# Attention and a gated feed-forward block: two written orders of steps joined into one, with buffers and banks named at each step

## The chip, the cores and the metric

The kernel runs on one core of a Trainium2 chip. The metric is device time in microseconds of one execution. A core has a matrix engine (TensorE, here PE, with its weight loads shown apart as PEld), VectorE (DVE), ScalarE (ACT) and GpSimd (POOL), and SyncE (SP), which issues the DMA transfers. Each engine works through its own queue in program order; an instruction waits in its queue until the instructions of other engines that it depends on have finished.

## The reference

The input is `q`, `k`, `v` of shape (8, 8, 576, 64): 8 batches, 8 heads, 576 positions, 64 features. Keys and values are averaged over groups of 8 positions, so each head attends to 72 of them. The result, as 4608 tokens of 512 features, goes through RMS normalization and a gated feed-forward block with 1536 inner features.

```python
k_p = k.reshape(B, H, Sp, pool, D).mean(axis=3)
v_p = v.reshape(B, H, Sp, pool, D).mean(axis=3)
scores = scale * np.matmul(q, k_p.transpose(0, 1, 3, 2))
attn = softmax(scores)
x = np.matmul(attn, v_p)            # then as (4608, 512)
xn = x / np.sqrt(np.mean(x * x, axis=-1, keepdims=True) + 1e-06) * rms_g
g = xn @ w_gate
out = (g * (1.0 / (1.0 + np.exp(-g))) * (xn @ w_val)) @ w_out
```

`softmax(scores)` stands here for the four lines that subtract the maximum, take the exponential and divide by the sum.

## The kernel before

**Precision.** The weights arrive as 64-bit numbers. Each is taken apart into a high and a low part, both in the 32-bit format that the profile calls fp32r, and activations are split in the same way. A product of two such numbers takes three matmuls: high by high, high by low, low by high.

**Tiling.** The 4608 tokens form 9 blocks of 512 (block 0 to 8). The 1536 inner features are 12 slices of 128, written in base 36 (0 to b) in the names of steps. For block i and slice f there are three groups of twelve matmuls with 512 columns each:

- `mm1` for the gate (L802 to L813, step `mg` or `_g`) and for the value (`me` or `_e`), into one PSUM bank each,
- `mm2`, the output product (L840 to L853, `mo` or `_o`), which adds into four banks that belong to the block for all its twelve slices.

Between them stand `gate` (`gt`, ACT: Silu out of the bank), `val` (`vl`, DVE: times the value bank), `act_hi` (`hi`, ACT: high part) and `act_lo` (`lo`, DVE: low part). `hl` and the activation `act` have one buffer each, `hh` has two.

Blocks 5 and 6, and 7 and 8, are computed in pairs by a scheme with seven products instead of eight (L752 to L764, `pr`): for each slice, seven groups of six matmuls, with sums and differences of activations (`ys`, `yh`, `yl`) and of weights. The parts of the weights (`wd`, `wt`, `wf`, `wh`, `wl`, `ws`) are prepared during earlier blocks, stored to device memory, and each comes back by a DMA into one of eight ring buffers just before its product (`rl`, L741 to L750). Ahead of `mo` for the second block of a pair (6 and 8), the first block's `mo`, in two halves (`mp`), is mixed with the products. The steps `cp`, `u2`, `sa`, `u3`, `c2`, `sw`, `v2`, `v1`, `va`, `vb` combine the products on ACT and DVE.

**Attention** of batch b, head pair p: loads (`lk`, `lq`, `lv`), pooling (`pk`, `pv` on DVE), scores on PE (`sc`, two banks), maximum and difference (`mx`, `sb`, DVE), exponential (`ex`, ACT), sums (`sm`, DVE), division (`nm`, POOL), a transposition (`tr`, DVE) with twelve small DMAs that place its parts (`dm`), the value product on PE (`av`, two halves), copies (`xc`, `xd`), squares (`sq`, `jn`). When a batch is done, sums of squares (`sh`, `sl`, `rm`), roots and scaling (`rt`, `rc`, `rs`) follow. Batches 0 and 1 take a path of their own, with transposes on PE; their steps are single letters.

**The order.** Nothing reorders the instructions: `manual_schedule` emits the steps as they are written. There are two written orders. `ORDER` (L52) holds batch 0, the splitting of all weights (`l` to `h`, `w`, `W`), block 0 and batch 1. Then a loop copies block 0's four output tiles and stores them. Then `LATER` (L88) holds everything else. The function `run` (L871) reads a step, a colon and bank numbers if there are any: `sc20:01` puts the scores in banks 0 and 1. Without a number a step has a fixed bank: the gate 2, the value 3, a block's output 4 to 7, products 2 and 3.

**Buffers.** Tiles of the pool `sb2` have two buffers, used in turn. The ring's eight buffers are used in turn as well. A step that takes a buffer or a bank waits for the last reader of what lay there before. `o_copy` (`ev`, L855: DVE for tiles 0 and 2, ACT for 1 and 3) copies an output tile out of its bank into one of the two `out` buffers, and `o_store` (`st`) issues the transfer.

Of the kernel before, what the change touches and what calls it, by code (L numbers as in the profile page):

```python
# [85 lines left out]


LATER = """  # L88
lv21 sc20:01 kt1 mg10 lk21 mx200 sb200 mx201 ex200 sb201 me10 gt10 sm200 nm200 ex201 mg11 vl10 hi10 sm201 lo10 nm201
me11 pv21 gt11 pk21 tr20 lq21 mo10 vl11 lv22 dm20 hi11 lo11 mg12 sc21:01 gt12 me12 mx210 sb210 mx211 ex210 lk22  # L90
sb211 mo11 vl12 ex211 sm210 hi12 lo12 nm210 sm211 av200:0 pk22 av201:1 nm211 xc200 mg13 lq22 xc201 xd20 tr21 sq20
pv22 dm21 me13 gt13 sc22:01 wt0 vl13 hi13 mo12 mx221 sb221 wf00 lo13 ex221 wf01 lk23 mx220 mg14 wf02 sb220 wh01
sm221 wf03 ex220 wd0 wh03 sm220 wl01 lv23 nm221 ws01 av210:0 gt14 nm220 pk23 av211:1 wl03 me14 lq23 xd21 xc210 ws03
xc211 mo13 vl14 hi14 pv23 wh04 wl04 mg15 lo14 ws04 wh02 wl02 sc23:01 ws02 sq21 tr22 gt15 jn21 me15 dm22 mx230 sb230
mx231 ex230 sb231 mo14 vl15 ex231 sm230 hi15 lo15 nm230 sm231 mg16 nm231 lk30 tr23 me16 gt16 dm23 av220:0 vl16
av221:1 pk30 xc220 hi16 mo15 xd22 xc221 sq22 lo16 jn22 mg17 lq30 lv30 wt1 me17 gt17 wf10 sc30:01 vl17 wd1 wf11 wh11
hi17 pv30 wl11 mo16 lk31 wh13 wf12 ws11 mx301 lv31 wl13 lo17 wf13 ws13 mx300 mg18 sb300 sb301 ex300 av230:0 ex301
sm300 gt18 av231:1 sm301 nm300 me18 xd23 nm301 pk31 xc231 xc230 pv31 lq31 wh14 wh12 wl14 mo17 vl18 wl12 ws14 hi18
ws12 tr30 sq23 jn23 lo18 mg19 dm30 sh2 sl2 me19 gt19 rm21:0 vl19 rm20:1 rt21 mo18 hi19 rc21 rt20 mg1a lv32 rs21
av300:0 lo19 av301:1 xc300 rc20 gt1a me1a xd30 rs20 xc301 sq30 wt2 sc31:01 vl1a mo19 lk32 mx311 hi1a wf20 mx310 wf21  # L100
lo1a wh21 wf22 wh23 sb310 mg1b wl23 sb311 wd2 ex310 pv32 wf23 ws23 wl21 pk32 ex311 ws21 sm310 me1b gt1b lq32 sm311
nm310 nm311 mo1a tr31 xh22 xh21 xl22 dm31 xh20 xl21 xh23 xl20 wh22 wh24 wl22 xl23 sc32:01 wl24 vl1b kt2 mg20 mx320
hi1b sb320 lo1b ex320 mx321 sb321 me20 lk33 gt20 lv33 sm320 ws22 ws24 nm320 ex321 mo1b vl20 hi20 pk33 lo20 lq33
av310:0 sm321 ev13 av311:1 xc310 st13 ev12 nm321 mg21 xc311 xd31 st12 sq31 pv33 jn31 tr32 sc33:01 ev11 gt21 st11
ev10 dm32 me21 mx330 sb330 mx331 ex330 sb331 mo20 vl21 ex331 sm330 hi21 wt3 sm331 lo21 mg22 nm331 st10 nm330 lk40
wf30 me22 gt22 wd3 wf31 tr33 wf32 wh31 dm33 wf33 wh33 av320:0 vl22 wl33 av321:1 xc320 pk40 wl31 hi22 mo21 xd32 xc321
lo22 mg23 lq40 me23 ws33 gt23 ws31 mo22 vl23 hi23 lo23 wh32 wh34 av330:0 wl32 av331:1 xc330 wl34 ws32 mg24 xc331
xd33 ws34 sq32 lv41 jn32 sc40:01 gt24 lv40 me24 lk41 mx400 sb400 mx401 ex400 sb401 pv41 mo23 ex401 vl24 sq33 sm400
hi24 jn33 pv40 mg25 nm400 sh3 lo24 sl3 pk41 me25 gt25 wt4 sm401 lq41 rm30:0 vl25 nm401 rm31:1 rt30 mo24 wf40 tr40
wf41 hi25 rc30 dm40 wf42 rt31 mg26 wh41 wf43 wh43 wl41 lo25 wl43 rs30 sc41:01 gt26 rc31 me26 rs31 wd4 mo25 lk42 ws41  # L110
vl26 ws43 mx411 hi26 sb411 mg27 lo26 ex411 mx410 sb410 ex410 sm411 av400:0 gt27 sm410 nm411 av401:1 nm410 me27 xd40
pk42 xc401 xc400 lq42 sq40 wh42 wh44 wl42 mo26 vl27 wl44 ws42 hi27 ws44 tr41 lv42 sc42:01 lo27 dm41 mg28 mx420 mx421
sb421 sb420 ex421 pv42 me28 gt28 sm421 nm421 mo27 ex420 vl28 lk43 hi28 sm420 lv43 wt5 mg29 lo28 pk43 nm420 av410:0
lq43 gt29 wf50 av411:1 wf51 me29 wd5 xd41 xc410 wf52 pv43 xc411 wh53 wf53 wh51 wl53 sq41 sc43:01 vl29 wl51 ws53 hi29
jn41 ws51 mo28 mx431 lk50 mx430 lo29 mg2a wh52 wl52 wh54 wl54 ws52 ws54 tr42 me2a gt2a sb431 dm42 pk50 ex431 sb430
mo29 vl2a ex430 sm431 hi2a sm430 nm431 lo2a mg2b nm430 tr43 me2b dm43 gt2b mo2a xh33 vl2b xh31 xl33 xh32 xl31 xh30
# [840 lines left out]
```

## Time and profile before

| | |
|---|---|
| time, median of 3 runs | 1022.78 us (1021.83 to 1024.94) |
| span of the profiled execution | 1024.9 us |
| first large matmul of block 0 starts at | 52.39 us |
| last matmul ends at about | 1019.1 us |
| mean granted clock of TensorE | 0.976 |

The profile is that of one execution. The page gives busy time for each engine, the span in slices, the chain of work that ended last, and the costliest groups of instructions. A group is named by its line, engine and operation, what it writes and what it reads (`po<-w,hl` writes `po`), then its count, its busy time, the mean duration of one in ns, and how long its engine was idle just before, with what ended that wait. Matmuls are pipelined, so their durations overlap: the time of one is read from the spacing of their starts.

The large matmuls of a slice all have 512 columns. The profile's lines for them are L811 (`psg`), L852 (`po`) and L763 (`px`, `py`). Attention on PE is L389 (`pss`, scores) and L470 (`psx`, value product).

```
DVE  7899996554783955685485486644655764444432
ACT  6757664553473564454364453322324431211121
PEclk8689999999999999999999999999999999999999
```

These three rows of the page show the span in 40 slices of 25.6 us: busy tenths of DVE and ACT, and the tenths of TensorE's full clock that were granted.

### The profile page before, as it was taken

To read this page: it belongs to the slowest core of one execution; us is meant where nothing else is said; L and a number is where in the kernel's file an instruction comes from. 1 tells how busy PE (TensorE), PEld (TensorE's weight loads), DVE (VectorE), ACT (ScalarE), POOL (GpSimd) and SP (SyncE) were. 2 spreads that over 40 slices of the span, in tenths; PEclk is the share of its full clock that TensorE was granted. 3 is DMA by queue.
4 is the path that set the end of the run, shared out by engine and by line. 5 is a ranking of instruction groups with operands and counts; after the bars stand their busy time and mean duration, and the time that the engine had idled before them with its cause. 6 is when DMAs were issued, how large, how long until landed. Compare 5 with 4: busy or idle time off the path is not lost.

```text
span 1024.9 us, 13861 instructions
## 1 busy us (share of the span) xinstructions
PE 992.1 (97%) x4850; PEld 790.8 (77%) x4850; DVE 632.3 (62%) x1024; ACT 449.7 (44%) x845; POOL 227.2 (22%) x216
## 2 busy tenths in 40 slices
...
DVE  7899996554783955685485486644655764444432
ACT  6757664553473564454364453322324431211121
...
PEclk8689999999999999999999999999999999999999
...
GB/s 313 121 166 180 176 75 58 79 147 139 68 175 136 79 179 104 152 119 145 111 138 154 123 90 105 173 199 153 147 160 147 42 113 154 151 153 149 103 41 42
DMA packets 97076, 134.71 MB, mean 131 GB/s; under 512 B 10224, under 2 KB 60144, under 8 KB 95728
## 3 DMA queue, kind: packets, MB, share of 16 engines
...
q8 instruction: 39, 0.64, 0.3%
...
## 4 chain that ended last, share of the span: by engine, by line
PE 86%; DVE 7%; ACT 3%; issue 1%; DMA 1%; SPq 0%; POOL 0%; ACTq 0%; DVEq 0%; POOLq 0%
PE psg L811 28%; PE po L852 27%; PE py L763 13%; PE px L763 10%; PE pss L389 4%; PE psx L470 3%; DVE wt L257 1%; DVE wt L261 1%; DMA main<-kT 1%; PE pst L446 1%; PE psr L554 1%; DVE hl L838 1%; DVE wt L253 1%; DVE xraw L546 0%; PE psb L578 0%
## 5 line engine op out<-in xcount | busy, mean ns | idle before, releaser
L811 PE MATMUL psg<-xh,w 128*128 128x512 f32 x960 | 304.2, 399 | 2.0 <-ACT act L818 2.0
L852 PE MATMUL po<-w,hh 128*128 128x512 f32 x864 | 225.1, 392 | 0.0
L811 PEld LDWEIGHTS psg<-xh,w 128*128 128x128 f32 x960 | 179.6, 190 | 48.4 <-issue 5.3
L852 PEld LDWEIGHTS po<-w,hh 128*128 128x128 f32 x864 | 163.5, 189 | 34.7
L811 PE MATMUL psg<-xl,w 128*128 128x512 f32 x480 | 188.0, 393 | 0.3 <-DVE xl L641 0.3
L763 PE MATMUL py<-xp,wp 128*128 128x512 f32 x576 | 146.5, 390 | 0.8 <-DVE u L913 0.8
L852 PE MATMUL po<-w,hl 128*128 128x512 f32 x432 | 125.2, 399 | 10.0 <-DVE hl L838 5.1
L763 PEld LDWEIGHTS py<-xp,wp 128*128 128x128 f32 x576 | 108.0, 188 | 24.1 <-DVE u L913 1.2
L763 PE MATMUL px<-xp,wp 128*128 128x512 f32 x432 | 110.2, 390 | 0.0
L811 PEld LDWEIGHTS psg<-xl,w 128*128 128x128 f32 x480 | 91.2, 190 | 20.4 <-DVE xl L641 0.7
L852 PEld LDWEIGHTS po<-w,hl 128*128 128x128 f32 x432 | 79.9, 189 | 32.6 <-DVE hl L838 6.7
L420 POOL TENSOR_TENSOR prob<-prob,sm 128x360 f32<-128x360 f32 x48 | 43.3, 903 | 275.8 <-DVE sm L416 267.5
L763 PEld LDWEIGHTS px<-xp,wp 128*128 128x128 f32 x432 | 80.8, 188 | 17.8 <-ACT xraw L478 0.5
L823 DVE TENSOR_TENSOR act<-act,psg 128x512 f32<-128x512 f32 x60 | 41.0, 683 | 77.4 <-PE psg L811 76.4
L833 ACT CAST hh<-act 128x512 fp32r<-128x512 f32 x84 | 52.1, 621 | 64.4 <-DVE act L823 55.8
L838 DVE TENSOR_TENSOR hl<-act,hh 128x512 fp32r<-128x512 f32 x78 | 57.1, 732 | 32.8 <-ACT hh L833 25.9
L818 ACT ACTIVATE act<-psg 128x512 f32<-128x512 f32 x60 | 35.9, 598 | 67.2 <-PE psg L811 63.6
L818 ACT ACT_TABLE_LOAD x34 | 43.6, 1283 | 33.8 <-DVE hl L838 17.8
L910 DVE TENSOR_TENSOR u<-u,py 128x512 f32<-128x512 f32 x24 | 16.5, 688 | 64.4 <-PE py L763 64.4
L515 POOL TENSOR_TENSOR acc<-acc,sq 128x576 f32<-128x576 f32 x21 | 31.4, 1497 | 99.9 <-ACT sq L509 92.9
L912 ACT ACTIVATE hb<-hb 128x512 f32<-128x512 f32 x24 | 15.2, 632 | 85.8 <-DVE hb L911 85.8
L685 POOL TENSOR_TENSOR wt<-wsum,wt 128x256 fp32r<-128x256 f32 x48 | 38.9, 825 | 51.9 <-ACT wt L681 51.8
(132 smaller groups left out, 1220.8 us busy)
## 6 DMA issues: line engine op xcount, KB each, us to landing
...
```

Of the source, the lines that this page charges most:

```text
L389: nc.tensor.matmul(s["ps", h][:, t * SP:(t + 1) * SP], s["q"][r, o:o + P], s["pk"][r, :], start=True, stop=True)
L420: nc.gpsimd.tensor_tensor(l_pr(h), l_pr(h), sm[:, :, None].broadcast_to([P, len(OFFS2), SP]), ALU.mult)
L470: nc.tensor.matmul(ps[r, :n], s["pv"][:, r], x, start=True, stop=True)
L515: nc.gpsimd.tensor_add(acc[b], acc[b], st[b, p]["sq"])
L685: nc.gpsimd.tensor_sub(y[:, 1], place(f, f"T{k}"), y[:, 0].bitcast(F32))
L763: nc.tensor.matmul(ps[:, :NB], w[:, a, c, :], x[:, b, c, :], start=j == 0 and not more, stop=j == len(todo) - 1, skip_group_check=more)
L811: nc.tensor.matmul(ps[:, :NB], w[:, c, cols], x[c], start=(j == 0), stop=(j == len(todo) - 1))
L818: nc.scalar.activation(t, ps[:, :NB], AF.Silu)
L823: nc.vector.tensor_mul(t, t, ps[:, :NB])
L833: nc.scalar.copy(a, act_in(i, f))
L838: eng.tensor_sub(l, act_in(i, f), hh[i, f].bitcast(F32))
L852: nc.tensor.matmul(po[i][t], x[i, f][:, t * P:(t + 1) * P], w, start=(f == 0 and k == 0), stop=(f == NF - 1 and k == 2))
```

## The change

The two orders become one. Steps that were in `ORDER` have an underscore in front, and the loop behind it is replaced by the steps `ev00` to `ev03` and `st00` to `st03`, which stand among the others. The steps as such, 2,593 of them, are the same before and after. Up to `_g0` of block 0 the order is the same; behind it, it is another. Steps of the two former orders are mixed where block 0 ends.

A step can now name a bank behind a colon for every use of PSUM that has one, `mg` and `me`, products and a block's four output banks too; and behind a slash which of two buffers (or of the ring's eight) its tile takes. The pool `sb2` is gone: `two` takes a tile of `sb1` whose tag ends with the named number.

So that steps of two slices or two blocks can lie between each other, gate, value, activation and product results are kept by block and slice and no longer by "the last one"; and `tokens` takes a block's kept tail only for positions within it.

The loader, the interpreter and the records:

```diff
-    sb2 = ctx.enter_context(tc.tile_pool(name="sb2", bufs=2))
+    taken = []
+
+    def two(shape, dt, tag, name):
+        return sb1.tile(shape, dt, tag=f"{tag}{taken.pop(0)}", name=name)
...
-        w = ring[i, f, k] = sb1.tile([P, 2, 2, P], F32R, tag=RING[len(ring) % len(RING)], name=f"wp{i}_{f}_{k}")
+        w = ring[i, f, k] = sb1.tile([P, 2, 2, P], F32R, tag=RING[int(taken.pop(0))], name=f"wp{i}_{f}_{k}")
...
-        if k in (0, 4):
-            st["X"] = bank(2, f"px{i}_{f}_{k}")
-        elif k in (1, 3, 5):
-            st["Y"] = bank(3, f"py{i}_{f}_{k}")
-        ps = st["Y"] if k in (1, 3, 5, 6) else st["X"]
+        if k in (0, 1, 3, 4, 5):
+            st["XY", i, f, k] = bank(2 if k in (0, 4) else 3, f"pxy{i}_{f}_{k}")
+        ps = st["XY", i, f, {2: 0, 6: 5}.get(k, k)]
...
-        ps = st["psg", 0]
-        t = st["act"] = sb1.tile([P, NB], F32, tag="act", name=f"act{i}_{f}")
+        ps = st["psg", i, f, 0]
+        t = st["act", i, f] = sb1.tile([P, NB], F32, tag="act", name=f"act{i}_{f}")
...
         for step in order.split():
+            step, _, free = step.partition("/")
+            taken[:] = free
             step, _, banks = step.partition(":")
             given[:] = [int(x) for x in banks]
             steps[step[:n]](*(int(x, 36) for x in step[n:]))
...
-        run(ORDER, 1, steps)
-        for t in range(NB // P):
-            o_copy(0, t)
-            o_store(0, t)
...
-        first_phase()
-        later_phase()
+        nc.sync.dma_start(gcol, gain)
+        run(ORDER, 2, {**{"_" + k: v for k, v in first_steps().items()}, **later_steps()})
```

The order where block 0 goes over into block 1, before and after:

```
ORDER: ... Fa B11:1 H10 ia o9 H11 K20 V20 q20 gb:2 La eb:3 Gb oa Fb ib jb t0 t1 t2 t3 ob
       (o_copy and o_store of block 0, tiles 0 to 3)
LATER: lv21 sc20:01 kt1 mg10 lk21 mx200 sb200 mx201 ex200 sb201 me10 gt10 sm200 nm200 ex201 mg11 vl10 hi10 sm201 ...

after: ... _gb _r1 _s1 _B10 _dp _q20 _B11:1 wd5 wd4 _eb _H10 _H11 _ho _wo _La _oa _Gb _Fb sc20:03 _t3 _t0 _t2 wd8
       _t1 _hp mg10 _v20/0 _wp _ib/1 _jb gt10 mx200/1 sb200 lk21 pk21/0 lv21/1 lq21 _ob ev01/1 ev00/0 st01 _V20/0
       ex200 sm200/1 me10:0 vl10 hi10/1 mx201/1 nm200 mg11 st00 sb201 ex201 sm201/1 ev02/0 sc21:01 lo10 me11 ev03/1
       gt11 mo10:5467 ...
```

In the middle, behind slice 5 of block 1 and slice 2 of block 2:

```
before: me15 dm22 mx230 sb230 mx231 ex230 sb231 mo14 vl15 ex231 sm230 hi15 lo15 nm230 sm231 mg16 ... me16 gt16 ... mo15
after:  me15 vl15 me16:0 hi15/0 kt1 tr23/0 lo15 av221:3 xc221 gt16 xd22 mo15
before: me22 gt22 wd3 wf31 tr33 wf32 wh31 dm33 wf33 wh33 av320:0 vl22 wl33 av321:1 xc320 pk40 wl31 hi22 mo21 ... mo22
after:  me22:0 lk40 gt22 av321:1 tr33/1 vl22 hi22/1 lo22 wh33/0 wl33 dm33/0 mg23:3 gt23 av320:2 wf32 xc321 mo22
```

Where block 5 goes over into block 6, and block 7 into block 8:

```
before: pr5b6 av730:0 rl710 v15b av731:1 va5b xc730 xc731 xd73 hi5b sq73 lo5b jn73 mo5b hi60 lo60 sh7 sl7 mo60 hi61
        ev52 ev51 ev50 st52 ev53 st51
after:  pr5b6 av731 xc731 mp5a0 v15b va5b hi5b/1 av730:3 xc730 mp5a1 xd73 sq73/0 jn73 sh7/1 lo5b sl7 mo5b ev52 hi60/0
        rm70:3 lo60 ev53 st53 ev51 ev50 st50 hi61/1 lo61 rm71:1 st52 rt71 rc71 mo60:6470

before: mp7a0 sa7b pr7b3 pr7b4 u37b pr7b5 c27b sw7b mp7a1 v27b vb7b pr7b6 v17b va7b hi7b lo7b mo7b hi80 lo80 mo80 hi81
        ev72 ev71 ev70 st72 ev73 st71
after:  pr7b4:3 lo7a pr7b5:1 c27b v27b mp791 rl7b6/4 pr7b6 v17b pr7b2 mp7a0 sa7b mp7a1 va7b hi7b/1 sw7b lo7b mo7b
        hi80/0 lo80 mo80:2103 ev72 hi81/1 lo81 mo81
```

In the products, an excerpt of slice 2 of block 7:

```
before: pr720 rl730 v171 va71 pr721 rl731 cp72 hi71 pr722 lo71 rl732 u272 mp710 rl733 sa72 pr723 pr724 rl734 u372 pr725
after:  pr720 rl716/2 pr716 mp701 rl721/4 cp72 rl722/5 pr721:1 v171 va71 pr722 hi71/0 lo71 sa72 rl723/6 mp710 pr723:0
        sw71 rl732/2 rl724/4 pr724 rl725/5 u272 pr725
```

More of the change, by code (lines that the diff above doesn't have):

```diff
@@ new lines @@
+_B11:1 wd5 wd4 _eb _H10 _H11 _ho _wo _La _oa _Gb _Fb sc20:03 _t3 _t0 _t2 wd8 _t1 _hp mg10 _v20/0 _wp _ib/1 _jb gt10
+mx200/1 sb200 lk21 pk21/0 lv21/1 lq21 _ob ev01/1 ev00/0 st01 _V20/0 ex200 sm200/1 me10:0 vl10 hi10/1 mx201/1 nm200
+mg11 st00 sb201 ex201 sm201/1 ev02/0 sc21:01 lo10 me11 ev03/1 gt11 mo10:5467 nm201 tr20/0 mx210/0 vl11 mx211/1 sb211
+ex211 wdb lk22 hi11/0 lo11 mg12:3 sb210 ex210 gt12 sm211/1 nm211 st03 wda st02 pv21/1 dm20/1 pk22/0 _J10 me12:1
+sm210/0 mo11 av200/0 xc200 nm210 lv22/1 mg13 lq22 vl12 tr21/0 wd1 wd6 av201:1 hi12/0 xd20 dm21/0 lo12 pv22/0 gt13 me13
@@ new lines @@
+rl5a2/7 u359 c259 v259 sw59 pr596 v159 pr592 sa59 vb59 sc73:01 va59 hi59/0 mx731/1 sb731 ex731 mx730/0 sb730 rl5a0/3
+pr5a0 cp5a ex730 rl5a3/6 rl5a4/5 pr5a1 u25a rl5b1/3 sm731/1 pr5a4:1 nm731 lo59 pr5a3:0 rl5a5/2 rl5b2/6 u35a sm730/0
+nm730 pr5a2 sa5a c25a sw5a pr5b1 pr5a5:0 v25a mp590 rl5a6/7 pr5a6 rl5b0/3 pr5b0 tr73/1 cp5b rl5b3/2 mp591 v15a va5a
+u25b rl5b4/0 vb5a pr5b3:1 u35b hi5a/0 pr5b4:0 rl5b5/1 pr5b5:1 c25b lo5a dm73/0 pr5b2 sa5b v25b pr5b6 av731 xc731 mp5a0
+v15b va5b hi5b/1 av730:3 xc730 mp5a1 xd73 sq73/0 jn73 sh7/1 lo5b sl7 mo5b ev52 hi60/0 rm70:3 lo60 ev53 st53 ev51 ev50
@@ L71 @@
+v27a mp790 vb7a rl7a6/4 pr7b0 cp7b pr7a6 v17a va7a hi7a/0 pr7b1:1 u27b pr7b3:0 u37b rl7b4/1 pr7b4:3 lo7a pr7b5:1 c27b
+v27b mp791 rl7b6/4 pr7b6 v17b pr7b2 mp7a0 sa7b mp7a1 va7b hi7b/1 sw7b lo7b mo7b hi80/0 lo80 mo80:2103 ev72 hi81/1 lo81
+mo81 hi82/0 lo82 mo82 hi83/1 ev73 lo83 mo83 hi84/0 ev70 lo84 mo84 hi85/1 lo85 hi86/0 st72 mo85 lo86 mo86 ev71 hi87/1
+lo87 hi88/0 mo87 lo88 hi89/1 st70 lo89 mo88 hi8a/0 mo89 vb7b st73 hi8b/1 lo8a mo8a st71 lo8b mo8b ev80 ev82 ev83 st83
+st80 ev81 st81 st82
 """
@@ L85 @@
 AHEAD = 12
[L88 to L98, printed above, removed]
@@ L164 @@
-rl700 pr5b4 rl701 u35b rl702 rl703 rl704 pr5b5 c25b rl705 sw5b mp5a1 rl706 v25b vb5b pr5b6 av730:0 rl710 v15b
-av731:1 va5b xc730 xc731 xd73 hi5b sq73 lo5b jn73 mo5b hi60 lo60 sh7 sl7 mo60 hi61 ev52 ev51 ev50 st52 ev53 st51
-lo61 st50 st53 rm71:0 hi62 rm70:1 mo61 rt71 lo62 rt70 rc71 mo62 hi63 lo63 rc70 mo63 hi64 lo64 rs70 mo64 hi65 lo65
-rs71 mo65 hi66 ys73 yh72 yh71 lo66 yl72 mo66 hi67 yh73 lo67 yl71 yh70 mo67 hi68 yl70 lo68 ys74 mo68 hi69 lo69 yh74
-yl73 mo69 hi6a yl74 lo6a ys76 mo6a hi6b lo6b yh76 ys75 mo6b yl76 yh75 yl75 pr700 ev61 ev63 st61 pr701 st63 cp70
@@ L184 @@
-u27b mp7a0 sa7b pr7b3 pr7b4 u37b pr7b5 c27b sw7b mp7a1 v27b vb7b pr7b6 v17b va7b hi7b lo7b mo7b hi80 lo80 mo80 hi81
-ev72 ev71 ev70 st72 ev73 st71 lo81 st70 st73 mo81 hi82 lo82 mo82 hi83 lo83 mo83 hi84 lo84 mo84 hi85 lo85 mo85 hi86
-lo86 mo86 hi87 lo87 mo87 hi88 lo88 mo88 hi89 lo89 mo89 hi8a lo8a mo8a hi8b lo8b mo8b ev83 ev82 ev81 ev80 st83 st82
-st81 st80
-"""
 EXP_SCALE = 1.0 / (POOL * float(np.sqrt(D)))
```

302 lines of the change are left out of this document (160 added, 142 removed).

## The prediction

> **What bounds the kernel now.** I read the page first: its busy line, then the idle time in part 5; then the table of 25 us stretches; then the chain of work that ended last, for the price of one group of matmuls; last the timeline, at the places where the chain leaves PE.
>
> ```profile
> span 1024.9 us, 13861 instructions
> PE 992.1 (97%) x4850; PEld 790.8 (77%) x4850; DVE 632.3 (62%) x1024; ACT 449.7 (44%) x845; POOL 227.2 (22%) x216
> PE 86%; DVE 7%; ACT 3%; issue 1%; DMA 1%; SPq 0%; POOL 0%; ACTq 0%; DVEq 0%; POOLq 0%
> ```
>
> PE is the bound: 86% of the chain, and no other engine above 62%. The profile page says that a busy PE is not PE at its peak, so the 97% does not limit the gain to 33 us; the matmuls have to be priced.
>
> ```profile
> 297.78 2.72 PE po L852 x12
> 300.50 1.12 PE psx L470 x8
> 301.62 2.98 PE psg L811 x12
> 304.61 1.27 PE pss L389 x20
> 305.88 2.94 PE psg L811 x12
> 802.40 29.97 PE po L852 x132
> ```
>
> These are pieces of the chain: start, length, group. Twelve matmuls of 512 columns take 2.72 us (0.227 each; 29.97/132 is the same). One head pair's scores (`sc`) take 1.27, its two value products (`av`) 1.12, and the first group of twelve behind either takes 0.22 to 0.26 more: about 0.25 for each change from attention to the feed-forward part.
>
> ```profile
> 75.00:100.00 25.00, 24.19 (x128) 18.91 (x127) 23.36 (x32) 18.68 (x43) 10.30 (x6) 1.00 0.59 195
> 100.00:125.00 25.00, 22.30 (x109) 17.75 (x108) 24.51 (x31) 16.50 (x38) 10.85 (x6) 0.93 0.45 148
> 125.00:150.00 25.00, 24.77 (x133) 18.70 (x132) 24.12 (x34) 16.33 (x40) 8.07 (x6) 1.00 0.20 67
> 175.00:200.00 25.00, 23.02 (x113) 18.51 (x110) 11.97 (x22) 13.12 (x19) 1.86 (x2) 0.93 0.37 114
> 375.00:400.00 25.00, 25.00 (x127) 19.86 (x126) 13.71 (x25) 11.98 (x20) 13.00 (x13) 1.00 0.48 147
> ```
>
> The columns are stretch, length, busy time (instructions) of PE, PEld, DVE, ACT and POOL, granted clock, DMA share, GB/s. The steady stretch from 375 loses nothing. PE loses time and clock where block 0 hands over to block 1 (175; two more such places below), and from 75 to 150, where DVE, splitting the weights, is busy for 72 of 75 us.
>
> ```profile
> 177.47 0.59 ACT L866 COPY o<-po 128x512 f32<-128x512 f32 x1 [3.68 <-DMA out<-o]
> 183.01 1.19 PE L811 MATMUL psg<-xh,w 128*128 128x512 f32 x2 [1.98 <-ACT act L818]
> 183.01 7.32 PE psg L811 x24
> 791.99 0.50 PE L852 MATMUL po<-w,hl 128*128 128x512 f32 x1 [1.76 <-DVE hl L838]
> 797.26 0.64 PE L852 MATMUL po<-w,hl 128*128 128x512 f32 x1 [2.26 <-DVE o L866]
> 797.26 4.61 PE po L852 x12
> 980.48 0.50 PE L852 MATMUL po<-w,hl 128*128 128x512 f32 x1 [2.88 <-DVE hl L838]
> 980.48 3.60 PE po L852 x10
> 986.11 0.50 PE L852 MATMUL po<-w,hl 128*128 128x512 f32 x1 [1.19 <-DVE o L866]
> L818 ACT ACT_TABLE_LOAD x34 | 43.6, 1283 | 33.8 <-DVE hl L838 17.8 <-PE psg L811 15.8
> ```
>
> These are the three joints, from timeline and chain, and one group of part 5. **Joint 1** (block 0 to 1): a wait of 1.98, then 24 matmuls in 7.32 where 5.44 is the price: 3.86 lost. Two output copies had waited for stores, the gate `gt10` stood behind them on ACT, and `mg11` needs its bank. **Joint 2** (`mo5b`, `mo60`): 1.76 + 2.26, then 4.61 for 2.72: 5.91. **Joint 3** (`mo7b`, `mo80`): 2.88 + 1.19, and 4.44 for 2.72 (the ten matmuls, and the rest up to 984.92, 1.19 before 986.11): 5.79. Together 15.56 us.
>
> **The change, part by part.** The diff is a reordering: before and after hold the same 2,593 steps, so no instruction is added or removed on PE, DVE, POOL or SP. What can change is waiting, the changes from attention to feed-forward, and table loads on ACT.
>
> *Joint 1.* `_ob` now stands behind `mg10`, and the output copies are steps: `ev01`, `ev00` behind `_ob`, `ev02`, `ev03` behind `mg11`. Between `mg10` and `mg11` PE has `_ob` and `me10`, 5.44; ACT needs a table load, 1.28, and `gt10`, some 0.6 like a cast of that size (L833, below), in that time. `ev02` and `ev03` wait for the stores of `ev00` and `ev01`, but those went out more than two PE groups earlier, against a wait of 3.68 when they went out just before. Behind `ev02` on DVE waits `lo10` (for `mo10`), behind `ev03` on ACT `gt11`; both have a PE group or more to spare. Cost left: nothing; at worst the old 3.86. The two stores on SP stand behind `lk21`, `lv21`, `lq21`, and behind them wait only loads of a later pair, `lk22` first.
>
> ```profile
> L823 DVE TENSOR_TENSOR act<-act,psg 128x512 f32<-128x512 f32 x60 | 41.0, 683 | 77.4 <-PE psg L811 76.4
> L833 ACT CAST hh<-act 128x512 fp32r<-128x512 f32 x84 | 52.1, 621 | 64.4 <-DVE act L823 55.8
> L838 DVE TENSOR_TENSOR hl<-act,hh 128x512 fp32r<-128x512 f32 x78 | 57.1, 732 | 32.8 <-ACT hh L833 25.9
> 791.88 1.43 POOL L515 TENSOR_TENSOR acc<-acc,sq 128x576 f32<-128x576 f32 x1 [17.44 <-ACT sq L509]
> 793.34 0.68 ACT L520 CAST sums<-acc 128x576 fp32r<-128x576 f32 x1 [1.03 <-POOL acc L515]
> 795.26 0.75 DVE L524 TENSOR_TENSOR sums<-acc,sums 128x576 fp32r<-128x576 f32 x1
> 790.28 0.37 ACT L478 COPY xraw<-psx 128x256 f32<-128x256 f32 x1 [0.17 <-PE psx L470]
> 790.68 0.23 DVE L483 COPY xraw<-psx 128x64 f32<-128x64 f32 x1
> 791.12 0.68 ACT L509 ACTIVATE sq<-xraw 128x576 f32<-128x576 f32 x1
> ```
>
> *Joint 2.* Behind `pr5b6` PE has `av731`, `mp5a0`, `av730`, `mp5a1`: 3.84. `mo5b` needs two DVE steps, a cast and a subtraction: 2 × 0.68 + 0.62 + 0.73 = 2.71, so it need not wait. `mo60:6470` takes bank 0 for one tile, and its first bank, 6, is copied out first. Its operand `lo60` stands on DVE behind `sl7` and `ev52`, and `sl7` waits for `av730`: 0.37 + 0.23 + 0.68 + 1.43 + 0.68 + 0.75, then a copy and a subtraction of 0.7 each, 5.5, against `mp5a1`, `mo5b` and a short sum on PE, 4.35. I leave 1.2, and 0.3 for hand-overs: 1.5 (from 0 to 5.91).
>
> *Joint 3.* `mo80:2103` takes banks that the products have left, so it no longer waits for the copies of block 7. `mo7b` needs `sa7b`, `va7b`, `hi7b`, `lo7b` after `pr7b2`: at the same prices 0.62 + 0.68 + 0.62 + 0.73 = 2.65, against `mp7a0` and `mp7a1`, 2.72. Left: 0.1 (to 2.9, if a hand-over slips).
>
> The slow matmuls go with the waits: each stretch lies right behind a wait of 1.2 to 2.9 us, and the stretch from 375, without such a wait, has a clock of 1.00. The Trainium skill (TensorE: Matmul & The Clock Gate, Part 1) has PE at half rate only after an idle window of about 3.4 us, and so would not put these stretches down to such waits. The trace disagrees: 1.98 us of idle time were enough. By that rule the 5.5 us of slow matmuls could stay; that is the second rival below.
>
> *Block 0 from 75 to 150.* Visible in PE's busy time: 0.81 + 2.70 + 0.23 us idle and 7% of clock for 25 us, some 5.5 in all. DVE has nearly the same list before each matmul group, so most stays. I added up the DVE steps that stand, in either order, before each group's last operand, and took off the PE groups before it: a group waits most where DVE's sum is furthest ahead. That is 17.8 us before (`_o4`) and 15.5 after (`_o3`), an estimate at the mean duration of each kind of step. I take 2.3 off (bounds: 3.1 worse, if the six `wd` transfers now issued in block 0 put off one weight load by a landing time, below; 5.5 better). DMA is at 0.20 to 0.59 here, which should hide them.
>
> *The middle.* Single waits there:
>
> ```profile
> PE po L852 <- DVE o L866: 4.8, 3, 2.3
> PE pss L389 <- ACT xraw L478: 0.8, 1, 0.8
> PE psg L811 <- DVE xl L641: 0.3, 1, 0.3
> ```
>
> Less the joints' 2.26 and 1.19, 2.5 us. The new order leaves `mo15` only 3.28 us of PE work behind `me15` and `mo22` 3.84 (5.44 was the least), against 0.68 + 0.62 + 0.73 = 2.03 of dependent work. I let old and new waits cancel: 0 (from 2.5 better to 10 worse).
>
> *Switches.* Counting the places where a feed-forward group follows an attention group gives 62 before, 75 after: 13 × 0.25 = 3.3 us more. They lie on PE itself, and nothing hides them.
>
> *Weight ring.* In the products, a ring slot now is named, and the part that takes it is needed sooner: 21 of 152 parts have three product groups, 4.08 us, from the slot's release to their use, where the least was 9.5 and the usual 12.24.
>
> ```profile
> 296.55 0.39 SPq L309 DMA_DIRECT2D k<-kT  x1
> 299.65 0.75 DVE L337 TENSOR_REDUCE pk<-k 128x72 f32<-128x576 f32 x1 [1.07 <-DMA k<-kT]
> 668.51 0.59 SPq L750 DMA_DIRECT2D wp<-blocks  x1
> 674.18 1.24 PEld L763 LDWEIGHTS px<-xp,wp 128*128 128x128 f32 x6 [0.49 <-DMA v<-vN]
> ```
>
> A load of about this size lands 3.1 us after its issue when it is alone, and 5.65 (I read the wait at 674.18 as one for the part issued at 668.51) behind a burst of twelve small placements. With 3.1 the 4.08 suffice: 0, the row of the case nearest to a steady ring. The upper end is a rival.
>
> *Table loads.* Changes between Exp, Silu and Sqrt on ACT fall from 82 to 71. ACT is 44% busy; outside the joints this gives nothing.
>
> **Sum**, on the profiled execution: 1024.9 − 15.56 + 1.6 − 2.3 + 3.3 = 1011.9. The span is at the upper end of the runs (1021.83 to 1024.94), and their median, 1022.78, is 2.1 below it, so I forecast 1009.8.
>
> **The rivals.**
>
> *Late weights (slower).* If parts land 5.65 us after issue, the 33 parts with less than that are late by 36 us together: 1046. For it: SP issues in order, and four sets of twelve placements stand among these parts. Against it: 14 of the 21 shortest leads are in the products of blocks 7 and 8, where no placements are left. It decides from a landing time of 4.7 us, where the deficits add up to 13, the whole gain.
>
> *Slow stretches stay.* If something other than the waits slows the matmuls, closing the waits leaves those 1.88 + 1.89 + 1.72 us standing: 1015.3. For it: joint 3's ten start at full speed and slow down within the group. Against it: three stretches, each behind a wait.
>
> *The waits move.* An order with less slack (`mo15`, `mo22`, `av` placed singly) puts a wait of 0.5 to 1 us behind every tenth of the 144 groups of blocks 1 to 4: 14 × 0.7, 10 more, 1020, within 0.3%.
>
> *Better.* The joints close fully, block 0 gains its 5.5 and the middle its 2.5: 1009.8 − 1.6 − 3.2 − 2.5 = 1002.5.
>
> **How the numbers follow.** Forecast 0.58, better 0.12, slow stretches 0.08, moved waits 0.15, late weights 0.07. 0.3%, about what a measurement of this kernel can tell from no change, is 3 us: under 1019.7, over 1025.8. Moved waits are half faster, half the same; hence faster 0.85, same 0.08, slower 0.07. The range runs from 1000 (the better case, and 2.5 for what its terms miss) to 1020, leaving out the late weights and the longer moved waits.
>
> **What would show it.** Right: no PE wait over 1.5 us behind `_ob`, `mo5b`, `mo7b` and `mo80`; clock 1.00 in the stretches at these joints; ACT table loads at 71; DVE still over 90% busy from 75 to 150. Wrong: PE or PEld idle at L763 with a DMA named; SP's queue long in front of L750; PE groups of 2.95 without attention before them; a wait on a copy L866 at the other blocks' first `mo`.

## The result: slower, and where the time went

The changed kernel takes 1036.58 us (median of 5 runs, 1034.47 to 1040.22) against 1024.94 for the kernel before on the same chip (5 runs, 1021.83 to 1027.36): a ratio of 1.0106, 95% interval 1.0068 to 1.0144. The forecast was 1009.8, with a range from 1000 to 1020. The profiled execution of the changed kernel spans 1033.6 us; before it was 1024.9. In the changed kernel the lines have moved: mm1 is L824 (L811 before), mm2 L865 (L852), the products L776 (L763), `sc` L404, `av` L485, the placements `dm` L448, the `wd` transfers L665.

First the page of the changed kernel: span, busy time, shares of the chain of waits.

```profile
span 1033.6 us, 13723 instructions
PE 1009.2 (98%) x4850; PEld 789.4 (76%) x4850; DVE 623.7 (60%) x1024; ACT 431.0 (42%) x834; POOL 228.2 (22%) x216
PE 89%; SPq 3%; DVE 2%; issue 2%; DMA 2%; ACT 1%; POOL 1%; POOLq 0%; ACTq 0%; DVEq 0%
```

PE is 17 us busier than before (992.1) with the same 4850 matmuls, so its idle time has shrunk by 8 us, and still the time has grown. Something makes the matmuls themselves longer. The table of 25 us stretches (columns as in the prediction) says the same:

```profile
125.00:150.00 25.00, 19.84 (x96) 15.30 (x97) 18.93 (x26) 12.95 (x35) 9.66 (x5) 0.86 0.47 144
200.00:225.00 25.00, 22.08 (x110) 15.49 (x109) 10.19 (x21) 7.22 (x13) 6.51 (x7) 0.97 0.52 146
800.00:825.00 25.00, 24.46 (x109) 18.72 (x109) 17.09 (x27) 12.54 (x22) 1.43 (x1) 1.00 0.29 96
850.00:875.00 25.00, 25.00 (x109) 20.32 (x108) 12.41 (x19) 5.23 (x10) 0.00 (x0) 1.00 0.45 138
975.00:1000.00 25.00, 24.57 (x106) 19.42 (x106) 11.25 (x17) 5.45 (x9) 0.00 (x0) 1.00 0.12 42
```

From 850 PE is busy for all of the 25 us at clock 1.00 and starts 109 matmuls. The kernel before, in the same stretch:

```profile
850.00:875.00 25.00, 25.00 (x112) 20.67 (x112) 11.34 (x17) 4.67 (x8) 0.00 (x0) 1.00 0.50 147
```

112. The timeline shows it within one group of twelve. Columns: start, length, engine, line, what. Each row holds two matmuls on `xh`; with the one on `xl` that stands between two rows, the start of a row is three matmuls behind that of the row above. Before:

```profile
388.73 0.61 PE L811 MATMUL psg<-xh,w 128*128 128x512 f32 x2
389.41 0.61 PE L811 MATMUL psg<-xh,w 128*128 128x512 f32 x2
390.09 0.61 PE L811 MATMUL psg<-xh,w 128*128 128x512 f32 x2
```

and the changed kernel:

```profile
386.06 0.63 PE L824 MATMUL psg<-xh,w 128*128 128x512 f32 x2
386.75 0.63 PE L824 MATMUL psg<-xh,w 128*128 128x512 f32 x2
387.46 0.63 PE L824 MATMUL psg<-xh,w 128*128 128x512 f32 x2
```

Three matmuls took 0.68 us; they take 0.69 to 0.71. From here on, **spacing** is the time from the start of one matmul of 512 columns to that of the next, from the records behind the timeline, spacings over 260 ns left out (waits, or attention between). Before, it is 227.9 ns on the mean for mm1, 227.5 for mm2 and 226.9 for the products; in the changed kernel 232.7, 229.1 and 232.6. Summed over 226.67 ns for each, that is 2.90 us before and 16.96 after: **14.1 us lost to pace**, with no wait anywhere.

By stage, with the pace apart. The differences count the last twelve matmuls of block 0, `_ob` (2.72 us), in block 0; the new order puts them behind the first matmuls of block 1. "Rest" is what remains when the pace is taken off.

| stage (from its first large matmul to that of the next) | before | changed | difference | of it pace | rest | forecast |
|---|---|---|---|---|---|---|
| start, to the first large matmul | 52.3 | 55.2 | +2.9 | | +2.9 | 0 |
| block 0 | 122.97 | 123.71 | +3.5 | 1.2 | +2.3 | -2.3 |
| blocks 1 to 4 (joint 1, middle, switches) | 459.29 | 467.85 | +5.8 | 5.9 | -0.1 | -0.6 |
| blocks 5 to 8 (joints 2 and 3, ring) | 384.09 | 380.91 | -3.2 | 7.0 | -10.2 | -10.1 |

The joints behave as forecast. Timeline of PE in the changed kernel, the longest wait at joint 2 and at joint 3, and the 24 matmuls of joint 1 from the chain:

```profile
810.62 0.50 PE L865 MATMUL po<-w,hl 128*128 128x512 f32 x1 [0.54 <-DVE hl L851]
994.84 0.50 PE L865 MATMUL po<-w,hl 128*128 128x512 f32 x1 [0.39 <-DVE hl L851]
184.68 5.60 PE psg L824 x24
```

Waits of 1.8 to 2.9 us have become 0.4 to 0.5, and with them the slow matmuls are gone: clock 1.00 from 800 and from 975, where 0.98 and 0.93 stood. Two long waits stand elsewhere now. Chain and timeline of the changed kernel:

```profile
130.16 1.07 PE L461 MATMUL pst<-ident,prob 128*72 128x128 f32 x4 [5.39 <-POOL prob L394]
131.23 4.54 PE po L865 x12
208.19 2.74 SPq L665
212.47 1.58 SPq L448
220.20 1.81 DMA pt<-sq
222.39 0.65 PE L485 MATMUL psx<-pt,pv 72*64 72x256 f32 x4 [2.29 <-DMA pt<-sq]
224.65 4.13 PE psg L824 x12
```

In block 0 PE waits 5.39 us for one step on POOL (at most 2.2 for a step of this kind before) and then runs twelve matmuls in 4.54 instead of 2.72. In block 1 SP issues `wd` transfers ahead of the placements of pair 21, PE waits 2.29 us for the placed data, and twelve matmuls take 4.13.

### The profile page after: what moved, and what is told of

Read it like the earlier page. It is cut to its first block, busy times and chain, and to the rows that moved or that the text cites. A ratio compares the mean times of both kernels' runs of the same rounds, so it can differ in the third digit from the quotient of the medians.

```text
span 1033.6 us, 13723 instructions
## 1 busy us (share of the span) xinstructions
PE 1009.2 (98%) x4850; PEld 789.4 (76%) x4850; DVE 623.7 (60%) x1024; ACT 431.0 (42%) x834; POOL 228.2 (22%) x216
## 4 chain that ended last, share of the span: by engine, by line
PE 89%; SPq 3%; DVE 2%; issue 2%; DMA 2%; ACT 1%; POOL 1%; POOLq 0%; ACTq 0%; DVEq 0%
PE psg L824 30%; PE po L865 27%; PE pxy L776 21%; PE pss L404 4%; PE psx L485 4%; SPq L448 2%; PE pst L461 1%; DMA main<-kT 1%; PE psr L569 1%; DMA wx<-w 1%; SPq L665 1%; DVE wt L268 1%; POOL prob L394 1%; PE psb L593 0%; DVE wt L276 0%
## 5 line engine op out<-in xcount | busy, mean ns | idle before, releaser
L824 PE MATMUL psg<-xh,w 128*128 128x512 f32 x960 | 305.9, 400 | 0.8 <-DVE act L836 0.8
L776 PE MATMUL pxy<-xp,wp 128*128 128x512 f32 x1008 | 243.0, 395 | 0.0
L865 PE MATMUL po<-w,hh 128*128 128x512 f32 x864 | 224.7, 392 | 0.0
L776 PEld LDWEIGHTS pxy<-xp,wp 128*128 128x128 f32 x1008 | 189.4, 188 | 45.3 <-issue 1.1
L824 PEld LDWEIGHTS psg<-xh,w 128*128 128x128 f32 x960 | 177.2, 189 | 51.5 <-issue 9.2
L865 PEld LDWEIGHTS po<-w,hh 128*128 128x128 f32 x864 | 163.0, 189 | 36.5 <-issue 0.8
L824 PE MATMUL psg<-xl,w 128*128 128x512 f32 x480 | 189.6, 396 | 0.0
L865 PE MATMUL po<-w,hl 128*128 128x512 f32 x432 | 126.4, 402 | 1.0 <-DVE hl L851 0.9
L824 PEld LDWEIGHTS psg<-xl,w 128*128 128x128 f32 x480 | 90.4, 188 | 21.8 <-DVE xl L656 0.4
L865 PEld LDWEIGHTS po<-w,hl 128*128 128x128 f32 x432 | 79.6, 189 | 24.8 <-issue 4.6
L435 POOL TENSOR_TENSOR prob<-prob,sm 128x360 f32<-128x360 f32 x48 | 40.6, 851 | 182.8 <-DVE sm L431 181.2
L851 DVE TENSOR_TENSOR hl<-act,hh 128x512 fp32r<-128x512 f32 x78 | 59.8, 767 | 30.7 <-ACT hh L846 30.4
L924 DVE TENSOR_TENSOR u<-u,pxy 128x512 f32<-128x512 f32 x24 | 16.5, 688 | 46.3 <-PE pxy L776 46.3
L404 PEld LDWEIGHTS pss<-pk,q 64*128 64x128 f32 x560 | 34.4, 192 | 10.2 <-issue 8.0
L425 ACT ACTIVATE prob<-prob 128x360 f32<-128x360 f32 x48 | 23.7, 504 | 43.3 <-DVE prob L421 43.2
L485 PE MATMUL psx<-pt,pv 72*64 72x256 f32 (+2 forms) x224 | 37.3, 428 | 4.3 <-DMA pt<-sq 2.5
```

The lines of the kernel that those rows point to most:

```text
L404: nc.tensor.matmul(s["ps", h][:, t * SP:(t + 1) * SP], s["q"][r, o:o + P], s["pk"][r, :], start=True, stop=True)
L435: nc.gpsimd.tensor_tensor(l_pr(h), l_pr(h), sm[:, :, None].broadcast_to([P, len(OFFS2), SP]), ALU.mult)
L485: nc.tensor.matmul(ps[r, :n], s["pv"][:, r], x, start=True, stop=True)
L776: nc.tensor.matmul(ps[:, :NB], w[:, a, c, :], x[:, b, c, :], start=j == 0 and not more, stop=j == len(todo) - 1, skip_group_check=more)
L824: nc.tensor.matmul(ps[:, :NB], w[:, c, cols], x[c], start=(j == 0), stop=(j == len(todo) - 1))
L851: eng.tensor_sub(l, act_in(i, f), hh[i, f].bitcast(F32))
```

## The experiments

Three questions: what slows the matmuls, what each of the two waits is worth, and whether the order is better than the old one without them. A pair of medians in one paragraph is from the same chip.

**Where the tiles stand.** The change turns the second pool (`sb2`, two buffers a name) into named buffers of the first. That moves tiles. In the built programs the start of each within a partition is, modulo 256 bytes:

```
                               before   changed
xh, xl (also the ring), acc, act  96      224
hh, hl                            96       96
w1, w2, product inputs xp         96       96
```

A `pk` tile is 96 floats, 384 bytes. Before, both stood together behind `xh` and ahead of `hh`, and two of them are three times 256 bytes. In the changed kernel one stands ahead of `xh`, so what follows is shifted by 128 modulo 256, until the other, ahead of `hh`, shifts it back. In mm1 the weights `w1` are loaded into PE and `xh`, `xl` stream through it; in the products the ring slots are loaded and `xp` streams. In both, the operands are now 128 bytes apart modulo 256. In mm2 (`hh`, `hl` loaded, `w2` streams) they aren't, but for the odd slices of blocks 6 and 8, whose `hl` stands in the buffer of `act`.

**e1_even**: one number of the changed kernel.

```diff
-            pk = two([P, 96], F32, tag="pk", name=f"pk{b}_{p}")[:, :SP]
+            pk = two([P, 128], F32, tag="pk", name=f"pk{b}_{p}")[:, :SP]
```

> The changed kernel, with one number altered: the pk tiles are allocated 128 floats wide (512 bytes) instead of 96 (384 bytes); what is computed in them stays in the first 72. In the built program the first pk tile stands ahead of xh, xl (which are also the ring slots), acc and act, so in the changed kernel these start 128 bytes past where the tiles they are multiplied with start, counted modulo 256 (224 against 96); with 512 bytes all of them are at 96, as in the kernel before. Nothing else differs: same steps, order, banks and buffers. In the changed kernel matmuls of 512 columns start 232.7 ns apart (mm1), 229.1 (mm2) and 232.6 (products); in the kernel before 227.9, 227.5 and 226.9; the difference adds up to 14.1 us over the groups. Placement theory (the offset of a matmul's two operands against each other sets its pace): spacings back at 227 to 228 in all three, the time 14 us lower, 1022 to 1023 us beside 1036.6 for the changed kernel. Order theory (the order, the named banks or the buffers themselves slow the matmuls): spacings stay at 229 to 233, the time stays at 1034 to 1040.

Measured: 1023.36 us beside 1026.6 for the kernel before, ratio 0.9958 (0.994 to 0.9976). Spacings 227.8, 227.5 and 226.8; sum over the base 2.69 us. The stretch from 850, e1_even:

```profile
850.00:875.00 25.00, 25.00 (x112) 20.72 (x111) 12.20 (x18) 5.19 (x9) 0.00 (x0) 1.00 0.56 179
```

112 again. Order, banks and buffers are those of the changed kernel, so none of them slows the matmuls.

**e2_odd**: the reverse, in the kernel before.

```diff
-            x = sb1.tile([P, 2, 2, 8], F32, tag=f"mxe{p}", name=f"mx{b}_{p}")
+            x = sb1.tile([P, 2 + 2 * (p == 3), 2, 8], F32, tag=f"mxe{p}", name=f"mx{b}_{p}")
...
-        t = st["act"] = sb1.tile([P, NB], F32, tag="act", name=f"act{i}_{f}")
+        t = st["act"] = sb1.tile([P, NB + 32], F32, tag="act", name=f"act{i}_{f}")[:, :NB]
```

> The kernel before, in its own order and with its own pools, but with 128 unused bytes ahead of xh, xl, acc and act and 128 more behind act, so that these four start at 224 modulo 256 and everything else stays at 96, as in the changed kernel. Placement theory: mm1 and products slow down to 232 to 233 ns between starts, mm2 to 228 or 229, and the time rises by about 14 us, to 1037 to 1040 beside 1024.9. Order theory: spacings stay at 227 to 228, the time within 3 us of before.

Measured: 1040.23 beside 1026.6, ratio 1.0135 (1.0105 to 1.0164). Spacings 232.9, 228.8, 232.8; 17.06 us over the base, 14.2 more than before. From 900 us, e2_odd:

```profile
900.00:925.00 25.00, 25.00 (x109) 20.32 (x108) 10.86 (x16) 4.67 (x8) 0.00 (x0) 1.00 0.47 146
```

128 unused bytes in two places cost 1.3%, in the old order. The two runs together show the cause of the 14 us.

**e3_all224**: e1_even, and everything large shifted by the same 128 bytes.

```diff
-    gcol = const.tile([P, NC], F32, name="gcol")
+    gcol = const.tile([P, NC + 32], F32, name="gcol")[:, :NC]
```

> As e1_even, and 128 unused bytes ahead of all large tiles, so that every operand of the large matmuls starts at 224 modulo 256: no two are offset against each other, but all stand where the slow ones stood. If the offset between the two operands matters, spacings are 227 to 228 and the time that of e1_even, 1022. If the place itself matters (224 is a bad place), all three kinds are slow, mm2 too, at 232 or more, and the time is 1037 to 1043.

Measured: 1023.15 beside 1026.6, ratio 0.997 (0.9952 to 0.9987); spacings 227.9, 227.5, 226.9. The place itself is harmless. What counts is the offset of one operand against the other.

**e4_d64, e9_d32, e10_d192**: other offsets, by the width of `pk` in the changed kernel.

```diff
-            pk = two([P, 96], F32, tag="pk", name=f"pk{b}_{p}")[:, :SP]
+            pk = two([P, 80], F32, tag="pk", name=f"pk{b}_{p}")[:, :SP]
```

(72 in e9_d32, 112 in e10_d192.)

> The changed kernel with pk tiles 80 floats wide (320 bytes): xh, xl, acc and act start at 160 modulo 256, 64 past the weights and product inputs at 96; hh and hl at 224, 128 past the w2 parts at 96. If an offset of 128 costs, mm2 now slows to 232 or 233 ns between starts (229.1 in the changed kernel, where both are at 96). mm1 and the products have an offset of 64: if any offset costs alike, 232 to 233; if only 128 does, 227 to 228. Time: 1024 to 1028 if 64 is harmless, 1038 to 1042 if it is not. Order theory: 1034 to 1040, mm2 at 229.

> The changed kernel with pk tiles 72 floats wide (288 bytes): xh, xl and the ring slots start at 128 modulo 256, 32 past their partners at 96; hh and hl at 160, 64 past the w2 parts. Measures the spacing of matmul starts for two more offsets. If only an offset of about half of 256 costs: mm1 and products at 227 to 229, mm2 (64) at 228 to 230. If any offset costs alike: all at 232 or more.

> The changed kernel with pk tiles 112 floats wide (448 bytes): xh, xl and the ring slots start at 32 modulo 256, 64 ahead of their partners at 96; hh and hl at 224, 128 past the w2 parts. In e4_d64, mm1 had its moving operand 64 past the weights and took 229.5 ns, the products their weights 64 past the moving operand and took 233.2. If the sign of the offset decides, the two change places here: mm1 at 233, products at 229.5; mm2 at 232.4 as in e4_d64. If the sign does not matter, mm1 stays at 229.5 and products at 233.

Measured: 1036.63 beside 1026.6 (e4_d64, ratio 1.0094, 1.0063 to 1.0124; 1038 to 1042 was forecast for an offset of 64 that costs); 1040.82 and 1035.27 (e9_d32, e10_d192), one run each, beside 1026.07 for the kernel before. Spacing in ns by the start of the loaded operand less that of the streaming one, modulo 256:

| loaded less streaming | spacing, and in which matmuls |
|---|---|
| 0 | 226.8 to 227.9 (all three kinds, before and e1_even) |
| 32 | 233.2 (products, e9_d32) |
| 64 | 233.1 (mm1, e10_d192), 233.2 (products, e4_d64; mm2, e9_d32) |
| 128 | 232.7 (mm1) and 232.6 (products), changed kernel; 232.4 and 232.5 (mm2, e4_d64 and e10_d192) |
| 192 | 229.5 (mm1, e4_d64), 229.2 (products, e10_d192) |
| 224 | 233.1 (mm1, e9_d32) |

The sign matters, as e10_d192 was to show: at 64 it is 233, at 192 (64 the other way) 229, for mm1 and products alike. "Only an offset of about half of 256" is out: in e9_d32 all three kinds are over 232. Over all runs "alike" does not hold exactly either: every offset tried costs, 192 less than the others. An offset of a multiple of 256 costs nothing: in the kernel before, `xh` for slice 0 starts at 168288 and `w1` of slice 0 at 104032, 251 times 256 apart. The Trainium skill (SBUF — State Buffer, Who interferes with whom) gives PE two independent read ports, one for the streaming operand and one for weight loads, and says that PE never waits on anyone. The trace disagrees as far as the independence goes: with the same work and no wait for another engine, 5 to 6 ns a matmul hang on how the addresses of the two operands lie to each other. Why they do, no run here shows.

**The queue on SP: e5_two.** On the base of e1_even, `wd1` and `wd6` behind `dm21`:

```diff
-tr21/0 wd1 wd6 av201:1 hi12/0 xd20 dm21/0 lo12
+tr21/0 av201:1 hi12/0 xd20 dm21/0 wd1 wd6 lo12
```

> e1_even with two steps moved: wd1 and wd6 (four DMAs of 512 KB) stand behind dm21 in the order instead of ahead of it; all else as in e1_even. There SP issues them from 203.4 to 208.8, the transposed probabilities of pair 21 are ready at 204.9, and their twelve placements go out from 208.9 to 218.5 (9.6 us; 7.7 where no large transfer is about); PE waits 2.2 us for the last of them and runs the next twelve matmuls in 4.37 instead of 2.72. Queue theory (the two steps on SP cause the wait): the placements start by 205.5, PE waits for none of them before 230, and the stretch from the first matmul of block 1 to the first of block 2, 119.9 us in e1_even and 120.4 in e3_all224, falls by 3 to 4.5; the time falls from 1023.4 to about 1019.5. Rival (the placements are late because the attention steps of pairs 20 and 21 come late, or because the DMA engines are full): the wait stays, the stretch stays at 119.5 to 120.5, the time within 1 us of e1_even.

Measured: 1022.32 beside 1027.44, ratio 0.9958 (0.994 to 0.9977). The wait for the placements is gone, but block 1 fell only from 119.9 and 120.4 to 118.56. The time did not fall: the ratio is that of e1_even, where about 1019.5 us was forecast. PE's waits from 55 us on show a new one:

```profile
PE psg L824 <- ACT act L831: 2.8, 1, 2.8
```

The two steps now hold up what stands behind them in the new place (e11_later).

**All twelve transfers back: e6_blocks, e7_first.** Both on e1_even; the order is changed only in the twelve `wd` steps, or in the first three.

```diff
-... _F3 wd0 _ca ... _F4 wd2 _i4/0 ... _V13/1 wd7 _S13:10 ...
+... ex220 wd0 ... sb311 wd2 ... sq50 wd7 ...
```

> e1_even with all twelve wd steps (24 DMAs of 512 KB) moved behind the steps behind which the kernel before has them, one about every 25 to 35 us from block 1 on; in the changed kernel all twelve are issued between 77 and 230 us, beside the weight loads of block 0 and the placements of block 1. Transfer theory: DMA share from 75 to 125 us falls from 0.8 and 0.6 to about 0.5, a weight load there lands in 4 us rather than 6.6, block 0 (first large matmul to the first of block 1; 122.3 in e1_even, 124.6 in e3_all224, 123.0 in the kernel before) falls to 119 to 121, block 1 to 116; time 1016 to 1018. Rival (block 0 is bound by the work on DVE, ACT and POOL, and the transfers are hidden): block 0 stays at 122 to 125, only block 1 gains its 3 to 4.5, time 1019 to 1020.

> e1_even with only wd0, wd2 and wd7, the three that are issued while block 0's weights are still being loaded, moved behind the steps behind which the kernel before has them; the other nine stay. Transfer theory: block 0 falls to 119 to 121, block 1 stays at 120, time 1020 to 1021. Rival (block 0 bound by DVE, ACT and POOL): both stay, time 1022 to 1024.

Measured: 1025.03 (ratio 0.9983, 0.9963 to 1.0003) and 1025.93 (0.999, 0.997 to 1.0011), both beside 1027.44. The transfer theory was right on blocks 0 and 1 and wrong on the time. In e6_blocks block 0 falls to 120.85 and block 1 to 115.41, as the transfer theory has it; but block 2 rises from 116.6 to 122.87 and block 3 from 113.8 to 116.99. SP's queue and PE's waits, e6_blocks:

```profile
373.89 1.32 SPq L665 DMA_DIRECT2D blocks<-w  x2
382.23 1.30 SPq L665 DMA_DIRECT2D blocks<-w  x2
383.63 1.28 SPq L332 DMA_DIRECT2D q<-qT  x1
PE pss L404 <- DMA q<-qT: 3.8, 2, 3.0
```

Two `wd` steps 8 us apart, then a load that is late by 3 us; the 48 matmuls behind that wait take 13.19 us instead of 10.88. Together that is 5.3 of the 6.3 us of block 2. The old places don't suit the new order. In e7_first block 0 is 121.02 and block 3 loses 3.3 us; what costs block 3 that, in both runs, was not traced. So the early transfers cost some 2.4 us in block 0 (the mean of e1_even, e3_all224 and e5_two is 123.4; with one profile each, these three lie 2.2 apart), but moving them without room elsewhere costs as much or more.

**The step on POOL: e8_norm.** On e5_two, one step on another engine:

```diff
-            N=lambda b, p, h: s_norm(b, p, h, G), T=s_pt,
+            N=lambda b, p, h: s_norm(b, p, h, V if (b, p, h) == (1, 2, 0) else G), T=s_pt,
```

> e5_two with one step of block 0 on another engine: the scaling of the probabilities of pair 2 of block 1, first head (step N120), runs on DVE instead of POOL. On POOL it takes 5.21 us in every profile of the new order so far (0.79 to 1.6 for the other fifteen steps of this kind), while DVE works through seven steps of the weight split without a gap; PE waits 5.4 us for it, and the next twelve matmuls take 3.83 instead of 2.72. Starvation theory (POOL's step is held up by DVE's, and PE waits for nothing else there): on DVE it takes 0.5 to 0.7, PE's wait behind it is under 1 us, block 0 (first large matmul to the first of block 1; 122.3, 124.6, 123.2 in e1_even, e3_all224, e5_two) falls to 117 to 119, the time by 4 to 6 us from 1022.3 to 1017 or 1018. Rival (the weight loads and ACT are as late there): another wait of 3 us or more takes its place, block 0 stays above 121, the time above 1020.

The rows behind it, timeline of DVE and POOL in e1_even:

```profile
121.22 1.47 POOL L851 TENSOR_TENSOR hl<-act,hh 128x512 fp32r<-128x512 f32 x1
121.47 1.25 DVE L388 TENSOR_SCALAR mx<-mx 128x5 f32<-128x5 f32 x1
122.86 0.65 DVE L467 COPY pt<-pst 72x512 f32<-72x512 f32 x1
123.02 5.21 POOL L394 TENSOR_TENSOR prob<-prob,mx 128x360 f32<-128x360 f32 x1 [0.33 <-DVE mx L389]
123.43 0.68 DVE L272 SCALAR_TENSOR_TENSOR wt<-wx,wt 128x512 uint32<-128x512 uint32 x1
124.03 0.68 DVE L294 TENSOR_TENSOR w<-wt,w 128x512 fp32r<-128x512 f32 x1
124.63 0.68 DVE L268 TENSOR_SCALAR wt<-wt 128x1024 uint32<-128x1024 uint32 x1
125.23 1.22 DVE L294 TENSOR_TENSOR w<-wt,w 128x1024 fp32r<-128x1024 f32 x1
126.36 1.22 DVE L272 SCALAR_TENSOR_TENSOR wt<-wx,wt 128x1024 uint32<-128x1024 uint32 x1
128.28 1.07 PE L461 MATMUL pst<-ident,prob 128*72 128x128 f32 x4 [5.44 <-POOL prob L394]
```

Beside POOL's step DVE works through six steps without a gap (the expectation says seven): a copy and five of the split. POOL's step ends 0.65 us after the last of them. The first two rows show the reverse: L388 on DVE, 0.16 us at 117.28 where POOL is idle, takes 1.25 beside a step on POOL. The Trainium skill (SBUF — State Buffer, Who interferes with whom) has a DVE instruction with two SBUF inputs contend with a POOL instruction that reads SBUF, over a shared pair of ports that it calls an exclusive lock; the trace agrees in so far as 5.21 us stand where the same kind takes 0.79 to 1.6 us elsewhere. Two inputs are not the whole of it: at 117.84 a POOL step of this kind took 1.58 while DVE ran L276, which reads two tiles in SBUF, without a gap.

Measured: 1015.35 beside 1026.07, ratio 0.9887 (0.9862 to 0.9912). Block 0 falls from 123.22 (e5_two) to 118.35, and PE waits 0.2 us for POOL in place of 5.6; a wait of 1.3 for the copy L467 on DVE, which now stands behind the moved step, is new. The starvation theory holds in its effect. That DVE's steps are what held POOL's up is read from the rows; no run changed them while the step stayed on POOL. Block 1 rises from 118.56 to 120.61. The medians of e5_two and e8_norm, from two chips, lie 7 us apart, the spans of the two profiled executions only 2.0 (1017.3 and 1015.3), so not all of the 7 us is accounted for.

**e11_later**: e8_norm with `wd1` and `wd6` where SP has little to issue.

```diff
-... xd20 dm21/0 wd1 wd6 lo12 ... jn22 dm23/0 wt1/0 ... dm30/1 wl14 ...
+... xd20 dm21/0 lo12 ... jn22 dm23/0 wd1 wt1/0 ... dm30/1 wd6 wl14 ...
```

> e8_norm with wd1 and wd6 moved once more: wd1 behind dm23, wd6 behind dm30, where SP has little to issue. In e8_norm (and e5_two) they go out right behind dm21, from 210.3 to 214.6; the first of four stores of weight sums behind them on SP goes out at 217.1 and lands at 221.3, ACT waits 6.0 us for its buffer, the gate (L831) stands behind that on ACT, and PE waits 3.4 us for it and runs the next twelve matmuls in 4.56. Queue theory (whatever stands behind the two steps on SP is late, first the placements, then the stores): neither PE's wait for placements nor that for the gate appears before 260, the stretch from the first matmul of block 1 to the first of block 2 falls from 120.6 (e8_norm) to 115 to 117, the time from 1015.4 to 1010 to 1012. Rival (the wait moves again, or comes from the other wd steps): the stretch stays above 118.5, the time above 1013.5.

The chain, SP's queue and ACT in e8_norm:

```profile
210.32 4.29 SPq L665 DMA_DIRECT2D blocks<-w  x4
217.09 4.25 DMA sum<-wt
221.42 0.41 ACT L696 CAST wt<-wsum 128x256 fp32r<-128x256 f32 x1 [6.01 <-DMA sum<-wt]
223.79 4.56 PE psg L824 x12
```

and the stretch from 200 in e11_later:

```profile
200.00:225.00 25.00, 25.00 (x141) 19.02 (x140) 13.02 (x23) 10.20 (x19) 11.34 (x12) 1.00 0.46 137
```

Measured: 1012.29 beside 1027.5, ratio 0.9857 (0.9829 to 0.9886); block 1 at 115.47. Waits and stretch are as the queue theory had them (141 matmuls where the changed kernel started 110), and the time is 0.3 us over its 1010 to 1012. With 32 floats, one engine and two steps altered, the new order is 1.4% faster than the kernel before.

## Why the prediction was wrong

**The failed step is the first one: the price.** "Twelve matmuls of 512 columns take 2.72 us (0.227 each)", with "no instruction is added or removed on PE", and "what can change is waiting, the changes from attention to feed-forward, and table loads". The prediction read a price from the kernel before and kept it for a kernel whose buffers lie elsewhere. The section on the change tells that the pool `sb2` is gone; the prediction gave that no cost, and no reason why it should have none. The price is 0.2267 only while the two operands start at the same place modulo 256 bytes, and the change moved `xh`, `xl` and the ring by 128: 14.1 us, shown both ways (e1_even, e2_odd). That is the larger part of the miss, 14.1 of 21.7 us by the profiles, and not all of it: with the pace of before, e1_even still takes 1023.36 us, over the range that was forecast.

**Block 0** was sized with the wrong sign: 2.3 gained, 2.3 lost beside the pace. The list of DVE's work ahead of each matmul group was drawn up with mean durations; it had no term for POOL being held up by DVE. That wait is 5.4 us and the slow matmuls behind it 1.8; with the step on DVE block 0 is 4.9 us shorter (e8_norm). The bound of 3.1 for the `wd` transfers was of the right size: some 2.4 (e6_blocks, e7_first).

**Joints 2 and 3 and the ring**: 10.1 forecast, 10.2 measured. 1.5 were left at joint 2 and 0.1 at joint 3 by forecast, 0.54 and 0.39 by trace. The slow matmuls went with the waits, so "slow stretches stay" falls. The idle window of about 3.4 us of the Trainium skill (TensorE: Matmul & The Clock Gate, Part 1) is again not borne out: 4.13 us for twelve matmuls stand soon behind a wait of 2.29 (granted clock 0.97 and 0.96 in the stretches from 200 and 225). No product waits for a DMA (idle 0.0 in front of L776): late weights did not come, and the 5.65 us of that rival (5.67 by its two rows) did not matter.

**Joint 1, the middle and the switches** came out at -0.1 against -0.6, but by two errors that cancel: the near hit is luck. Joint 1 closed. The two `wd` steps on SP cost 4 to 5 us in block 1, ahead of `dm21` as well as right behind it (119.9 in e1_even and 120.6 in e8_norm, 115.5 in e11_later), a price that the text looked for only in the weight loads of block 0 and, as late weights, in the products. Without them there blocks 1 to 4 gain 5.0 instead of 0.6 (456.98 in e11_later, less 2.72, against 459.29); so the 3.3 for the switches and the 0 for the middle were together 4.4 too high.

**The start** is no effect of the order: the first large matmul comes between 52.2 and 56.3 us in all thirteen profiles, and at 52.3 and 55.4 in the two that have the old order. **From profile to median**, 2.1 us were taken off because a span was held against run times; but a run takes about 1.9 us more than its span (1035.55 against 1033.6 here), and the kernel before has a median of 1027.44 over 29 later runs. The forecast should have been 1011.9 + 1.9.

The sum closes on the profile: 14.1 for the pace, 4.6 for block 0, 2.9 for the start and 0.5 for blocks 1 to 4 are 22.1, less 0.1 for the joints, 22.0; 1033.6 - 1011.9 is 21.7, and the difference is rounding and the last stores.

Of the signs to look for, the first three were right (no PE wait over 1.5 us at the four places, clock 1.00 there, 71 ACT table loads, and so 834 ACT instructions against 845), and they said nothing of the time. "DVE over 90% busy from 75 to 150" was wrong: 86% up to 125 (21.42 and 21.48 of 25 us) and 76% behind it. Long groups without attention before them were listed as a sign against, with 2.95; they came, at 2.80 in mm1 (5.60 for 24 at joint 1).
